# Mixture of experts behind an mLSTM: rows ahead of weights in the load queue, one transposition and one turn moved

## The chip, the core and the metric

The kernel runs on one core of a Trainium2 chip. A core has five engines that run side by side and wait for each other through semaphores: TensorE (PE in the rows; its weight loads are PEld), VectorE (DVE), ScalarE (ACT), GpSimd (POOL) and SyncE (SP), whose queue issues most of the transfers; 16 DMA engines carry them out. Each engine takes its instructions strictly in the order in which they were written. The metric is device time in microseconds (us); lower is better.

## What is computed

```python
def _moe_ref(x, token_ids, w1, w2):          # N, D, E, F = 3072, 320, 8, 1024
    expert_idx = token_ids * np.int64(2654435761) % np.int64(E)
    for e in range(E):
        mask = expert_idx == e
        xe = x[mask]
        h = np.maximum(xe @ w1[e], 0.0)
        out[mask] = h @ w2[e]
```

`x` (3072 tokens of 320) is the output of an mLSTM over 4 batches of 8 heads with 768 steps and head size 40. Everything is in 32-bit floats. The change lies wholly in the part with the experts.

## The kernel before, in words

The program has two parts. The first (0 to about 129 us) computes the mLSTM in 24 chunks of 128 tokens and writes the rows of `x` to a table in memory (`x_rows`); beside it the tokens are sorted by expert into index tables. The second part runs the eight experts, numbered here 0 to 7 as in the code, so that the fourth expert is expert 3.

An expert has 416 places for tokens: three blocks of 128 and a remainder of 32. Its rows take this way. `fetch(e)` gathers three blocks from `x_rows` with three indirect transfers that GpSimd issues (tile `xg`), and SyncE's queue stores them in a second table in memory (`x_slots`). `blocks(e)` loads them back as 12 small transfers on the same queue, in such an order that VectorE can turn rows into columns with one instruction, STREAM_TRANSPOSE in `turned(e)` (from tile `xb` to `xT`). The remainders of four experts are gathered at once, for experts 0 and 4. Expert 0 goes another way: its rows are transposed on TensorE in `turn` (two transpositions, a small VectorE copy at L891, a third transposition, then a copy out of the accumulators), the first two blocks already in the first part, the third block and the remainder in `turns0`.

`load_weights(e)` puts four transfers on SyncE's queue: `w1t`, two of `w1c`, `w2t`. The first layer of experts 1 to 7, `layer1_by_seven`, multiplies with seven products in place of eight and needs sums of weights (`sw`, by `sums_of_w1`, VectorE) and differences of rows (`tx`, by `sums_of_x`, VectorE); it works in two halves, `g` 0 and 2, and calls `meanwhile(g)` in the middle of each. The second layer takes the third block with `layer2` and the first two with `layer2_by_seven`, which calls its own `meanwhile` after its first four products. VectorE adds the partial results in both layers, ScalarE copies and applies the maximum, GpSimd scatters the results to the output.

The order of all work is that of the code: there is no scheduler in this part. SyncE's queue goes from top to bottom too, and a transfer that waits for a semaphore holds all that stand behind it. A block load waits until the store of its expert's rows has landed in memory.

The pools have `xg`, `xb`, `xT` and `tx` in two copies each, and the weights of the first layer in one early and two late places.

Of the kernel before, what the change touches and what calls it, by code (L numbers as in the profile page):

```python
# [22 lines left out]
def kernel(  # L23
# [30 lines left out]
    E, _, F = moe_w1.shape  # L54
    FB = F // P
# [32 lines left out]
    s_idx = consts.tile([P, NC], I32, name="s_idx")  # L88
# [25 lines left out]
    W = {}  # L114

    def load_weights(e, eng=None):

        W[e] = weights(moe_w1[e], moe_w2[e], wpools[e % 3 > 0], w2pools[e % 6 > 0], eng)
# [72 lines left out]
    with tc.tile_pool(name="gates", bufs=1) as gp, \  # L191
# [174 lines left out]
        def turn(s, what):  # L366
            d = st[s]
            d[what + "T"] = wk.tile([P, PR, P], F32, name=what + "T", bufs=3)
            tp = ps.tile([P, PR, P], F32, name="tr", tag="tr", bufs=2)
            for j in range(PR):  # L370
                nc.tensor.transpose(tp[:, j, :], d[what][:, 2 * j : 2 * j + 2, :].rearrange("p h d -> p (h d)"), ident[:])  # L371
            nc.scalar.copy(d[what + "T"][:], tp[:])
# [498 lines left out]
    def scatter(zp, idx, apart):  # L871
        zo = xp.tile([P, Dm], F32, name="zo", bufs=4)
        nc.scalar.copy(zo[:], zp[:])  # L873
        scatter_rows(zo, idx, apart)
# [111 lines left out]
                nc.scalar.activation(o, o, AF.Relu)  # L986
            done(g)

    def layer2(w, h, js, idx, apart, between=lambda j: None):
        for j in js:  # L990
            zp = mps.tile([P, Dm], F32, name="zp")
            for fb in range(FB):
                nc.tensor.matmul(  # L993
                    zp[:], lhsT=h[:, fb, j * P : (j + 1) * P], rhs=w[2][:, fb, :],
                    start=(fb == 0), stop=(fb == FB - 1),
                )
            scatter(zp, idx(j), apart)
            between(j)

# [56 lines left out]
    def cols_of(t, c0):  # L1056
        return lambda j: t[:, c0 + j : c0 + j + 1]

    with tc.manual_schedule():
        xTs, hrem, xbs = {}, {}, {}  # L1060
        xr0 = xp.tile([P, DB * P], F32, name="xr0", bufs=1)
        xTs[0] = xT0

        def fetch(e):
            if e == 0:
                gather(xg0[:, 2, :Dm], cols_of(g_idx, 0)(2))
                gather(xr0[:, :Dm], cols_of(g_idx, NR)(0))
            else:
                xg = xp.tile([P, NJ, Dm], F32, name="xg")
                for j in range(NJ):  # L1070
                    gather(xg[:, j], cols_of(g_idx, e * NJ)(j))
                nc.sync.dma_start(xs_d[e, :NM].rearrange("(t p) d -> p t d", p=P), xg[:])
            if e % EG == 0:
                if e:
                    xr = xp.tile([P, Dm], F32, name="xrg", bufs=1)
                    gather(xr[:], cols_of(g_idx, NR + e // EG)(0))
                else:
                    xr = xr0[:, :Dm]
                nc.sync.dma_start(xs_d[e : e + EG, NM:], xr[:])

        def blocks(e):
            xb = xbs[e] = xp.tile([P, CAP // 32, DB, 32], F32, name="xb")
            rows = xs_d[e].rearrange("(g j) d -> j g d", j=32)
            for q in range(4):
                for c in range(DB):
                    d0 = c * P + (q if c + 1 < DB else q % 2) * 32
                    nc.sync.dma_start(xb[q * 32 : (q + 1) * 32, :, c], rows[:, :, d0 : d0 + 32])  # L1087

        def turned(e):
            xT = xTs[e] = xp.tile([P, DB, CAP], F32, name="xT")  # L1090
            nc.vector.transpose(xT.rearrange("p c (g j) -> p g c j", j=32), xbs.pop(e)[:])

        def turns0():
            turn(xg0[:, 2], xT0[:, :, 2 * P : NM], False)
            remT = xp.tile([P, DB, P], F32, name="remT", bufs=1)
            turn(xr0, remT[:], True)
            nc.gpsimd.tensor_copy(xT0[:, :, NM:], remT[:, :, :RM])

        def rest(g):
            zp = mps.tile([P, Dm], F32, name="zp")  # L1100
            for fb in range(FB):
                for i in range(EG):
                    nc.tensor.matmul(  # L1103
                        zp[i * RM : (i + 1) * RM, :], lhsT=hrem[g][:, i, fb, :], rhs=W[g * EG + i][2][:, fb, :],
                        start=(fb == 0), stop=(fb == FB - 1),
                    )
            scatter(zp, cols_of(s_idx, NR + g)(0), True)

        fetch(0)
        fetch(1)  # L1110
        blocks(1)
        load_weights(1)
        h = h0
        for e in range(E):
            g, i = e // EG, e % EG
            if e + 2 < E:
                fetch(e + 2)
                blocks(e + 2)
                if e == 0:
                    load_weights(2)  # L1120
            if i == 0:
                hrem[g] = xp.tile([P, EG, FB, RM], F32, name="hrem")
            if e == 0:
                layer2(W[0], h, range(2), cols_of(s_idx, 0), True, lambda j: j == 0 and turns0())
                layer1(W[0], xT0, h, 2 * P, CAP, bank)
                turned(1)
                tx = sums_of_x(xTs[1])
            else:
                tw = differences_of_w2(W[e])
                sh = xp.tile([P, 4, FB // 2, P], F32, name="sh", bufs=1)  # L1130
                layer1_by_seven(
                    W[e], sw, xTs[e], tx, h, lambda g: g == 0 and 1 < e < E - 1 and turned(e + 1),
                    lambda g: sums_of_h(h, sh, g, nc.vector if g else nc.gpsimd),
                )
            nc.gpsimd.tensor_copy(hrem[g][:, i], h[:, :, NM:])
            layer2(W[e], h, (2,), cols_of(s_idx, e * NJ), True)
            if e + 1 < E:
                sw = sums_of_w1(W[e + 1])
            if i == EG - 1 and e + 1 < E:
                rest(g)  # L1140
            if e > 0:
                txs = []

                def meanwhile():
                    if e == 1:
                        turned(2)
                    if e + 1 < E:
                        txs.append(sums_of_x(xTs[e + 1]))

                layer2_by_seven(W[e], tw, h, sh, cols_of(s_idx, e * NJ), meanwhile)  # L1150
                tx = txs[0] if txs else None
            if e + 1 == E:
                rest(g)
            if e + 3 < E:
                load_weights(e + 3)

    nx = nc.values_load(xe[0:1, NX : NX + 1], min_val=0, max_val=NX)
    with tc.If(nx > 0):
        with tc.For_i(0, nx, 1) as k:
# [4 lines left out]
            w = weights(  # L1164
                moe_w1[bass.ds(ex, 1)].rearrange("e d f -> (e d) f"),
                moe_w2[bass.ds(ex, 1)].rearrange("e f d -> (e f) d"), wpools[0], w2pools[0],
            )
# [36 lines left out]
```

## Time and profile before

| | |
|---|---|
| three runs, median (lowest to highest) | 374.46 us (374.02 to 374.75) |
| profiled execution, own time | 372.34 us |
| its span, first to last instruction | 370.5 us |
| TensorE busy | 344.5 us, 93% of the span |
| VectorE, ScalarE, GpSimd busy | 59%, 37%, 57% of the span |
| mean granted TensorE clock | 0.979 of full speed |

The profiled execution is one run; 1.84 us of its time lie outside its span. All times inside the program, in the rows below too, are counted from the start of the span. A busy share is a mean over stages with different limits, so what a change is worth must be read in its own stage.

### The profile page before, as it was taken

Reading aid. Unit: us, or ns where it says so; the run is one execution under the profiler, and the core shown is the slowest. Engines: PE = TensorE matmul, PEld = TensorE weight load, DVE = VectorE, ACT = ScalarE, POOL = GpSimd, SP = SyncE. Lnnn points to the kernel's source line nnn. Section 1 sums busy time; section 2 is a strip of 40 time slices with the busy share of each in tenths; the row PEclk is TensorE's granted clock in tenths of the full one; section 3 lists DMA queues with packets and bytes.
Section 4 is the critical chain, followed back from the end, with each engine's and each line's share of the span. In section 5 each row is a group of like instructions: output and inputs, shape, how many; then the busy total and the mean of one; then the engine's idle time right before and its main releaser. Section 6 shows DMA issues by size and latency. Waiting matters only on the chain.

```text
span 370.5 us, 9233 instructions
## 1 busy us (share of the span) xinstructions
PE 344.5 (93%) x3595; PEld 296.8 (80%) x3595; DVE 219.8 (59%) x508; ACT 138.2 (37%) x325; POOL 209.5 (57%) x299
## 2 busy tenths in 40 slices
PE   8899999999999897999990999999999999999990
PEld 7777888888888775889880889869889899899870
DVE  7567897998878620185641565635575666745310
ACT  6476688767666611114110311410422413212300
POOL 8432778898884665149257315923944927419221
PEclk9999999999999999999996799999999999999997
DMA  7699999999999835788998959484478331000010
GB/s 148 116 185 171 169 185 203 206 184 181 172 210 239 253 90 177 176 285 181 317 309 160 308 118 323 105 225 156 118 155 260 104 68 37 1 18 35 6 46 5
DMA packets 162483, 59.35 MB, mean 160 GB/s; under 512 B 140130, under 2 KB 158206, under 8 KB 162438
## 3 DMA queue, kind: packets, MB, share of 16 engines
q1 hardware_dynamic: 158310, 49.07, 57.6%
q0 software_dynamic: 2832, 9.34, 7.8%
q8 instruction: 29, 0.48, 0.5%
q10 hardware_dynamic: 1296, 0.33, 0.4%
q14 instruction: 16, 0.13, 0.1%
HBM read 46.57 MB, written 12.48 MB: 159 GB/s over the span
## 4 chain that ended last, share of the span: by engine, by line
PE 76%; issue 5%; DMA 5%; DVE 4%; SPq 3%; POOL 3%; ACT 1%; POOLq 0%; ACTq 0%; DVEq 0%
PE mh L951 19%; PE mh L1025 11%; PE zp L993 9%; PE sp L419 7%; PE mh L959 6%; PE tr L371 6%; PE xh L477 5%; DMA x_slots<-xg 3%; PE xh L471 3%; PE ab L382 3%; PE xh L450 2%; SPq L1087 2%; POOL xg L110 1%; PE mh L157 1%; PE zp L1103 1%
## 5 line engine op out<-in xcount | busy, mean ns | idle before, releaser
L877 POOL DMA_INDIRECT out_dram<-zo,s_idx x26 | 26.7, 1027 | 86.8 <-issue 47.6
L993 PE MATMUL zp<-w2t,h 128*128 128x320 f32 x160 | 44.8, 433 | 0.5 <-issue 0.5
L951 PE MATMUL mh<-tx,sw 128*128 128x208 f32 x168 | 34.1, 354 | 10.1 <-DVE h L937 10.1
L951 PEld LDWEIGHTS mh<-tx,sw 128*128 128x128 f32 x168 | 31.1, 199 | 11.2 <-DVE h L937 11.0
L937 DVE TENSOR_TENSOR h<-u,mh 128x416 f32<-128x416 f32 (+1 forms) x56 | 25.2, 474 | 24.6 <-PE mh L951 16.5
L993 PEld LDWEIGHTS zp<-w2t,h 128*128 128x128 f32 x160 | 30.1, 190 | 12.0 <-issue 0.9
L477 PE MATMUL xh<-v,w 128*64 128x41 f32 x768 | 34.6, 222 | 0.0
L425 DVE TENSOR_TENSOR w<-sp,w 128x512 f32<-128x512 f32 x48 | 30.7, 681 | 4.8 <-ACT w L386 4.8
L386 ACT ACTIVATE w<-ab 128x512 f32<-128x512 f32 x48 | 26.1, 597 | 17.6 <-PE ab L382 17.6
L419 PE MATMUL sp<-qT,kT 64*128 64x128 f32 x384 | 29.8, 285 | 1.8 <-DVE w L425 1.2
L477 PEld LDWEIGHTS xh<-v,w 128*64 128x64 f32 x768 | 30.6, 138 | 0.0
L419 PEld LDWEIGHTS sp<-qT,kT 64*128 64x128 f32 x384 | 24.5, 187 | 6.7 <-issue 3.1
L110 POOL DMA_INDIRECT xg<-x_rows,g_idx x24 | 23.3, 972 | 9.0 <-issue 6.7
L1025 PE MATMUL mh<-tw,sh 128*128 128x160 f32 x168 | 27.4, 299 | 0.0
L471 PE MATMUL xh<-C,qs 128*64 128x82 f32 x320 | 27.3, 249 | 0.0
L494 POOL TENSOR_TENSOR x<-x,og 128x320 f32<-128x320 f32 x24 | 20.6, 864 | 7.5 <-ACT og L411 5.4
L937 DVE TENSOR_TENSOR u<-m,mh 128x416 f32<-128x416 f32 x28 | 16.2, 587 | 14.2 <-PE mh L951 7.7
L951 PE MATMUL mh<-xT,w1t 128*128 128x208 f32 x112 | 24.6, 342 | 0.0
L1025 PEld LDWEIGHTS mh<-tw,sh 128*128 128x128 f32 x168 | 24.3, 190 | 0.0
L959 PE MATMUL mh<-xT,w1c 64*128 64x208 f32 x224 | 24.1, 350 | 0.0
L975 ACT ACTIVATE h<-mh 128x416 f32<-128x416 f32 x14 | 7.2, 517 | 41.3 <-PE mh L959 41.3
L873 ACT COPY zo<-zp 128x320 f32<-128x320 f32 x12 | 5.1, 425 | 47.0 <-PE zp L993 30.5
(237 smaller groups left out, 765.6 us busy)
## 6 DMA issues: line engine op xcount, KB each, us to landing
w2t<-in_moe_w_dram SPq DMA_DIRECT2D x7, 1280.0 KB
w1t<-in_moe_w_dram SPq DMA_DIRECT2D x7, 1024.0 KB
xb<-x_slots SPq DMA_DIRECT2D x84, 52.0 KB
k<-in_k_dram SPq DMA_DIRECT2D x24, 160.0 KB
v<-in_v_dram SPq DMA_DIRECT2D x24, 160.0 KB
og<-in_o_gate_dram SPq DMA_DIRECT2D x24, 160.0 KB
q<-in_q_dram SPq DMA_DIRECT2D x23, 160.0 KB
x_slots<-xg SPq DMA_DIRECT2D x7, 480.0 KB
```

Of the source, the lines that this page charges most:

```text
L110: nc.gpsimd.indirect_dma_start(out=xg, out_offset=None, in_=x_d[:rows, :], in_offset=bass.IndirectOffsetOnAxis(ap=idx, axis=0),)
L386: nc.scalar.activation(w[:, hf], ab[:], AF.Exp)
L419: nc.tensor.matmul(sp[hf][:, j, :], lhsT=d["kT"][r, j, :], rhs=d["qT"][r, j, :], start=True, stop=True)
L425: nc.vector.tensor_tensor(d["w"][:, hf], d["sp"][hf][:], d["w"][:, hf], op=ALU.mult)
L471: nc.tensor.matmul(xh[t, 2 * j : 2 * j + 2, :], lhsT=d["qs"][:, j, t], rhs=Cs[b][c % 2][:, j].rearrange("p h d -> p (h d)"), start=True, s ...
L477: nc.tensor.matmul(hs[t, 2 * j + hf, :], lhsT=d["w"][:, hf, j, t], rhs=d["v"][:, 2 * j + hf, :], start=(c == 0), stop=True, skip_group_che ...
L877: ins = nc.gpsimd.indirect_dma_start(out=out[:, :], out_offset=bass.IndirectOffsetOnAxis(ap=idx, axis=0), in_=zo[:], in_offset=None, bound ...
L937: nc.vector.tensor_tensor(o, a, b, op=ALU.add)
L951: nc.tensor.matmul(pair(bank[n])[:, a], lhsT=lhsT(g + a), rhs=rhs, start=first and a == 0, stop=True, skip_group_check=True,)
L959: nc.tensor.matmul(pair(bank[n])[:, a], lhsT=w1c[k, g + a, :], rhs=xT[k, 2, r], start=False, stop=True, skip_group_check=True,)
L993: nc.tensor.matmul(zp[:], lhsT=h[:, fb, j * P : (j + 1) * P], rhs=w[2][:, fb, :], start=(fb == 0), stop=(fb == FB - 1),)
L1025: nc.tensor.matmul(bank[n], lhsT=lhsT(f), rhs=rhs(f), start=first and f == 0, stop=f == FB // 2 - 1, skip_group_check=True,)
```

## The change

Three things are written differently. In the loop over the experts, the weights of expert e + 2 are loaded at the top of iteration e, right behind the rows of expert e + 2; before, the weights of expert e + 3 were loaded at the end of iteration e, which is ahead of the rows of that expert. The rows of expert 3 are turned in the second layer of expert 2 (as those of expert 2 were in that of expert 1), no longer in its first layer. The transpositions of the first remainder stand between the sixth and the seventh matmul of expert 0's second block, no longer ahead of that block.

```diff
-    def layer2(w, h, js, idx, apart, between=lambda j: None):
+    def layer2(w, h, js, idx, apart, between=lambda j: None, within=lambda j, fb: None):
...
                     start=(fb == 0), stop=(fb == FB - 1),
                 )
+                within(j, fb)
...
-        def turns0():
+        def turn_third():
             turn(xg0[:, 2], xT0[:, :, 2 * P : NM], False)
+
+        def turn_rest():
             remT = xp.tile([P, DB, P], F32, name="remT", bufs=1)
             turn(xr0, remT[:], True)
             nc.gpsimd.tensor_copy(xT0[:, :, NM:], remT[:, :, :RM])
...
                 fetch(e + 2)
                 blocks(e + 2)
-                if e == 0:
-                    load_weights(2)
+                load_weights(e + 2)
...
-                layer2(W[0], h, range(2), cols_of(s_idx, 0), True, lambda j: j == 0 and turns0())
+                layer2(W[0], h, range(2), cols_of(s_idx, 0), True, lambda j: j == 0 and turn_third(), lambda j, fb: (j, fb) == (1, FB - 3) and turn_rest())
...
-                    W[e], sw, xTs[e], tx, h, lambda g: g == 0 and 1 < e < E - 1 and turned(e + 1),
+                    W[e], sw, xTs[e], tx, h, lambda g: g == 0 and 2 < e < E - 1 and turned(e + 1),
...
                 def meanwhile():
-                    if e == 1:
-                        turned(2)
+                    if e < 3:
+                        turned(e + 1)
...
-            if e + 3 < E:
-                load_weights(e + 3)
-
```

On SyncE's queue, from the weights of expert 2 on, stood before (`xg_2939` and `xb_2944` are the rows of expert 3, the three groups of `w1t`, `w1c`, `w2t` the weights of experts 2, 3 and 4):

```order
L97 DMA w1t_2815<-in_moe_w1_dram 128x2x1024
L100 DMA w1c_2816<-in_moe_w1_dram 64x4x128 x2
L101 DMA w2t_2817<-in_moe_w2_dram 128x8x320
L97 DMA w1t_2932<-in_moe_w1_dram 128x2x1024
L100 DMA w1c_2933<-in_moe_w1_dram 64x4x128 x2
L101 DMA w2t_2934<-in_moe_w2_dram 128x8x320
L1072 DMA x_slots<-xg_2939 128x3x320
L1087 DMA xb_2944<-x_slots 32x13x32 x12
L97 DMA w1t_3132<-in_moe_w1_dram 128x2x1024
```

At the same place of the queue stands now (`xg_2932` and `xb_2937` are the rows of expert 3, `w1t_2950` begins its weights, `xg_3132` and `xrg_3137` are the rows of expert 4 and the second remainder):

```order
L97 DMA w1t_2815<-in_moe_w1_dram 128x2x1024
L100 DMA w1c_2816<-in_moe_w1_dram 64x4x128 x2
L101 DMA w2t_2817<-in_moe_w2_dram 128x8x320
L1073 DMA x_slots<-xg_2932 128x3x320
L1088 DMA xb_2937<-x_slots 32x13x32 x12
L97 DMA w1t_2950<-in_moe_w1_dram 128x2x1024
L100 DMA w1c_2951<-in_moe_w1_dram 64x4x128 x2
L101 DMA w2t_2952<-in_moe_w2_dram 128x8x320
L1073 DMA x_slots<-xg_3132 128x3x320
L1080 DMA x_slots<-xrg_3137 4x32x320
```

The store and the 12 loads of expert 3's rows moved ahead of the four transfers of its weights; everything up to the weights of expert 2 stands where it stood.

On VectorE, in the first half of expert 2's first layer, stood before:

```order
L937 TENSOR_TENSOR u2_3171<-m1_3170,mh_3167 128x416
L937 TENSOR_TENSOR u4_3172<-m1_3170,mh_3168 128x416
L937 TENSOR_TENSOR u4_3172<-u4_3172,mh_3169 128x416
L1091 STREAM_TRANSPOSE xT_3185<-xb_2944 128x13x3x32
L937 TENSOR_TENSOR h0_74<-u4_3172,mh_3167 128x2x208
L937 TENSOR_TENSOR h0_74<-u2_3171,mh_3168 128x2x208
```

The transposition of expert 3's rows stands now in the second layer of expert 2, behind the sums of expert 3's weights and three additions:

```order
L908 TENSOR_TENSOR sw_3273<-w1t_2950,sw_3273 128x512
L1040 TENSOR_TENSOR u2_3283<-m1_3282,mh_3279 128x160
L1040 TENSOR_TENSOR u4_3284<-u2_3283,mh_3280 128x160
L1040 TENSOR_TENSOR zo_3286<-u4_3284,mh_3281 128x160
L1092 STREAM_TRANSPOSE xT_3307<-xb_2937 128x13x3x32
L912 TENSOR_TENSOR tx_3309<-xT_3307 128x208
L913 TENSOR_TENSOR tx_3309<-xT_3307,tx_3309 128x208
```

So the additions of the first layer (L937) no longer stand behind a wait for expert 3's rows. On TensorE, in the second layer of expert 0, the difference is (`xr_2768` is the first remainder, `xg_72` the third block):

```order
 L890 MATMUL tp<-ident,xg_72 128x128 x2
 L892 MATMUL tp<-ident,xg_72 128x128
+L993 MATMUL zp<-w2t,h_74 128x320 x6
 L890 MATMUL tp<-ident,xr_2768 128x128 x2
 L892 MATMUL tp<-ident,xr_2768 128x128
-L993 MATMUL zp<-w2t,h_74 128x320 x8
+L993 MATMUL zp<-w2t,h_74 128x320 x2
 L157 MATMUL mh<-xT_73,w1t 128x160 x4
```

Six of the eight matmuls moved ahead of the remainder's transpositions, and two are left between these and the first layer of the third block, which reads what they turn.

## Rows read from the trace of the kernel before

**Rows 1.** The page: the span.

```profile
span 370.5 us, 9233 instructions
```

**Rows 2.** The chain that ended last, two pieces: start us, us, what.

```profile
179.80 12.90 DMA x_slots<-xg
...
200.34 2.06 DMA xb<-x_slots
```

**Rows 3.** Timeline, TensorE: start us, us, operation, count [idle before <- releaser].

```profile
144.17 0.27 PE L892 MATMUL tp<-ident,xg 128*128 128x128 f32 x1
...
146.44 0.33 PE L892 MATMUL tp<-ident,xr 128*128 128x128 f32 x1 [1.78 <-DVE xr L891]
...
150.91 1.25 PE L157 MATMUL mh<-xT,w1t 128*128 128x160 f32 x8
...
161.45 0.87 PE L951 MATMUL mh<-xT,w1t 128*128 128x208 f32 x4
162.15 2.27 PE L951 MATMUL mh<-tx,sw 128*128 128x208 f32 x12
...
186.82 0.87 PE L951 MATMUL mh<-xT,w1t 128*128 128x208 f32 x4
...
204.49 4.09 PE L951 MATMUL mh<-tx,sw 128*128 128x208 f32 x12 [10.07 <-DVE h L937]
...
224.24 0.87 PE L951 MATMUL mh<-xT,w1t 128*128 128x208 f32 x4
```

**Rows 4.** Timeline, VectorE: the turn of expert 3, the weight sums and turn of 2.

```profile
179.40 0.69 DVE L905 TENSOR_TENSOR sw<-w1t 128x512 f32<-128x512 f32 x1 [1.45 <-DMA w1t<-in_moe_w_dram]
...
184.23 1.48 DVE L1091 STREAM_TRANSPOSE xT<-xb 128x1248 f32<-128x1248 f32 x1
...
202.48 1.48 DVE L1091 STREAM_TRANSPOSE xT<-xb 128x1248 f32<-128x1248 f32 x1 [12.06 <-DMA xb<-x_slots]
```

**Rows 5.** Stretches of 2 us: engines' busy time, granted clock, DMA share, GB/s.

```profile
core 0: us, PE busy (x) PEld busy (x) DVE busy (x) ACT busy (x) POOL busy (x), PEclk, DMA share, GB/s
...
200.00:202.00 2.00, 0.00 (x0) 0.00 (x0) 0.00 (x0) 0.00 (x0) 1.67 (x2) 0.50 0.73 109
```

**Rows 6.** Timeline, SyncE's queue: start us, us that the issuing took.

```profile
153.55 0.56 SPq L97 DMA_DIRECT2D w1t<-in_moe_w_dram  x1
...
156.20 0.87 SPq L1072 DMA_DIRECT2D x_slots<-xg  x1
166.13 6.02 SPq L1087 DMA_DIRECT2D xb<-x_slots  x12
172.20 0.47 SPq L97 DMA_DIRECT2D w1t<-in_moe_w_dram  x1
...
174.66 0.83 SPq L97 DMA_DIRECT2D w1t<-in_moe_w_dram  x1
...
179.80 4.73 SPq L1072 DMA_DIRECT2D x_slots<-xg  x1
194.72 6.09 SPq L1087 DMA_DIRECT2D xb<-x_slots  x12
200.92 0.41 SPq L97 DMA_DIRECT2D w1t<-in_moe_w_dram  x1
...
213.52 6.06 SPq L1087 DMA_DIRECT2D xb<-x_slots  x12
```

**Rows 7.** Timeline, all engines: around the turn of the first remainder.

```profile
145.43 0.56 DVE L896 COPY xT<-tp 128x384 f32<-128x384 f32 x1 [6.77 <-PE tp L890]
...
146.12 0.26 DVE L891 COPY xr<-xr 128x64 f32<-128x64 f32 x1
...
146.80 0.48 ACT L894 COPY remT<-tp 128x384 f32<-128x384 f32 x1 [0.93 <-PE tp L892]
147.35 0.26 POOL L1097 COPY xT<-remT 128x96 f32<-128x96 f32 x1 [0.17 <-issue]
...
159.96 0.69 DVE L905 TENSOR_TENSOR sw<-w1t 128x512 f32<-128x512 f32 x1
```

## The prediction, made before the changed kernel ran

> **What bounds the kernel now.** I read the chain of work that ended last first. In the part with the experts it is TensorE nearly everywhere, with one large hole: it leaves TensorE for a store of gathered rows that takes 12.90 us to land, and comes back by a block load that lands 2.06 us after its issue [rows 2]. The reader is to see that the hole belongs to transfers and not to any engine's work. Then I read TensorE in time. It stands still for 1.78 us ahead of the remainder's last transposition in expert 0, and for 10.07 us in the first layer of expert 2; between the start of expert 1 (161.45) and that of expert 2 (186.82) lie 25.37 us, between that of expert 2 and that of expert 3 (224.24) 37.42 [rows 3]. Expert 1 does the same work as expert 2, so expert 2 loses 12.05 us, of which 10.07 are the hole and 1.82 come behind it: the first twelve products after it take 4.09 us where the same twelve of expert 1 take 2.27 [rows 3], since the granted clock is then at 0.50, the 1.2 GHz level [rows 5]. It fell inside the hole, in which TensorE did nothing from 194.42 on.
>
> VectorE says why: it waits 12.06 us in front of the transposition of expert 3's rows [rows 4], and the additions that would free TensorE's accumulators stand behind it. SyncE's queue says why the rows are late. Expert 3's store is issued at 179.80, behind the weights of experts 2 (from 172.20) and 3 (from 174.66); its block loads can start only at 194.72, when the store has landed, and take 6.09 us to issue [rows 6]. They are in place 1.67 us later, at 202.48 [rows 4].
>
> **The rows ahead of the weights.** Nothing moves on SyncE's queue up to the weights of expert 2 at 172.20, and nothing in that stretch waits for TensorE. The store then takes the place of expert 3's weights, 174.66. It still has one expert's weights ahead of it. This case is in the trace twice: weights from 153.55, a store behind them at 156.20, block loads at 166.13, which is 12.58 us from the first weight to the landed store; and 200.92 to 213.52, 12.60 us, with a remainder's store as well [rows 6]. So the store lands at 172.20 + 12.6 = 184.8, the block loads are issued until 190.9 (6.1 us) and in place at 192.6 (1.7). The upper bound for the landing is the present 12.90 us counted from 174.66, hence 187.6.
>
> The weights of expert 3 now begin at 190.9 (193.7 at the upper bound), 16 to 19 us later than before. Who waits for them first is `sums_of_w1` on VectorE in expert 2. In expert 1 VectorE was ready for it at 179.40 - 1.45 = 177.95, 16.5 us after the expert's start [rows 3, 4]; in expert 2, started at 186.82 less the 1.0 us won below, that is 202.3. A first weight transfer lands within 6.4 us (issued at 153.55, read without a wait at 159.96 [rows 6, 7]) to 7.2 us (172.20 to 179.40, with the next expert's weights pressing behind it [rows 4, 6]). So it is in place at 198.1, or 200.9 with both upper bounds: 4.2 or 1.4 us in hand. I take no cost. What hides it is TensorE's work in expert 2's first layer; without that cover each microsecond is lost in full, because the additions of the second layer stand behind the sums.
>
> The Trainium skill, "DMA: Bandwidth & Descriptors", section "Rules for kernel authors", advises to issue a DMA early and to wait for it late, which speaks against this step for the weights. By its fit in "Anatomy of one DMA" (2 us and the bytes over 436 GB/s) a load of 1024 KB would take an estimated 4.4 us, landing at 195.3: no cost either. The first rival below is what the advice warns of.
>
> **The turn of expert 3 in the second layer.** One VectorE instruction of 1.48 us [rows 4] moves from between the additions of the first layer to behind three additions of the second. Expert 1 already has such a turn there, at 184.23, 22.8 us after its start, and it takes the plain 25.37 us; so I cost it at nothing. It is hidden by the rest of the second layer's products. Behind it stand the four differences `tx` of expert 3 and two output additions; if the rows were not in place, TensorE would wait in expert 3's second group of products. They are wanted at 185.8 + 22.8 = 208.6 and there at 192.6: 16 us in hand. Even with the order of the transfers unchanged (202.48) the turn would find its rows; each of the two edits alone removes most of the hole.
>
> Sum of both: expert 2 takes expert 1's 25.37 us instead of 37.42, a gain of **12.05 us** (the hole, the slow clock behind it, and 0.16 us of VectorE's turn in the first layer).
>
> **The remainder's turn.** Now TensorE waits 1.78 us for the small copy at 146.12 [rows 3, 7]. Eight matmuls of the block lie between 146.44 and 150.91 with a transposition, so 0.54 us each [rows 3]. Six of them in front give VectorE 3.2 us, and the copy is done by then, in 146.38. The gain is at most 1.78 us. But VectorE's copy ahead of it began only at 145.43, 1.0 us after the record of the third block's last transposition ends (144.44) [rows 3, 7], and no row says what held it. If that also holds the matmuls, the gain is 146.44 - 145.43 = 1.0 us. On the other side, TensorE's next reader needs the remainder copied by ScalarE (to 147.28) and GpSimd (to 147.61), 0.84 us behind the last transposition at 146.77 [rows 3, 7]; two matmuls, 1.1 us, cover that where eight did. If GpSimd is just issuing a transfer, the cover breaks and up to 1 us goes. A third limit stands in expert 1: VectorE reads its first weights at 159.96 without a wait, but when they landed between 153.55 and then isn't shown, and their issue isn't moved; at worst the gain ends there. So 0 to 1.78; I take **1.0**, the value that the unexplained release points to.
>
> **Sum.** 12.05 + 1.0 = 13.05 us. The span of 370.5 [rows 1] becomes 357.45, the profiled execution's 372.34 becomes 359.3. The median of the runs shown, 374.46, lies 2.1 us above that execution; taken off it, the forecast is **361.4 us**. All later experts keep their time: from 224.24 on TensorE has no hole to win.
>
> **Rivals.**
> *The weights come late.* The sums of expert 3's weights take over the wait of the turn. For it: they are the tightest point, and were loaded an expert earlier until now. Against: 4.2 us in hand, by two equal cases. It decides when the store lands after 189.0; a landing at 192.7, as late as now, would cost 3.7 us: 365.1. Chance 0.12.
>
> *The wait moves to expert 4's rows*, which are still turned in a first layer. Turns there are wanted 3.6 us after the expert's start (202.48 - 12.06 = 190.42 against 186.82 [rows 3, 4]), so at 224.24 - 13.05 + 3.6 = 214.8. Their store stands behind expert 3's weights: 190.9 + 12.6 = 203.5, and 7.8 for the loads makes 211.3. In hand 3.5 us; with the late landing above, 0.7. If these stores take 5 us more, 1.5 us are lost: 362.9. Chance 0.06.
>
> *It does not do what it says*: the store stays blocked until the DMA engines are free of all weights, lands where it did, and the hole only changes its name. That would need both the sums and the turn to wait as long as now, which the two slacks speak against: 374.5. Chance 0.02.
>
> *Slower.* Each expert's weights now stand behind a store's landing and 12 loads, so the queue becomes a ring: weights, store, loads, 172.20 to 190.9, 18.7 us a round against TensorE's 25.37. It decides above 25.4 us; to lose the 13.05 gained and 0.75 more over the five experts 3 to 7, a round must take 25.4 + 2.8 = 28.2 us, half as long again as the rows show: 375.2 or more. Chance 0.03.
>
> **How the numbers follow.** The forecast's own range is 360.2 (both gains full, less the 0.4 us by which the runs differ) to 362.8 (no early gain), chance 0.77. To this come the two rivals of partial loss, up to 365.5; the low end goes to 359.0 for waits that also shrink when fewer weights press (VectorE's 1.45 us at 179.40). The range 359.0 to 365.5 leaves out about 0.1. Faster by over 0.2% (about what a measurement here can tell from no change) are the forecast and the first two rivals, 0.95; within 0.2% 0.02; slower 0.03.
>
> **What would show it.** Expert 2 takes 25.4 us between its first matmuls, with the granted clock at 1.00 throughout; the store of expert 3's rows is issued near 174.7 and its loads near 185; no wait of VectorE in front of expert 3's turn, which stands in the second layer; the weight sums of expert 3 start without a wait for `w1t`. Ahead of the remainder's last transposition the idle 1.78 us are gone, and expert 1 starts near 160.5. I am wrong if VectorE waits for `w1t` in expert 2, for `xb` in expert 3, or if TensorE waits for the remainder's copy before the third block's first layer.

## The result: 362.0 us, 0.967 of before, and the profile after

The changed kernel took 362.01 us (median of four runs, 361.77 to 362.46) beside 374.27 (374.02 to 374.75) for the kernel before, measured beside it: a ratio of 0.9672, 95% interval 0.9656 to 0.9689. Forecast were 361.4, and 359.0 to 365.5 as the range. Lines of the kernel after stand up to three lower than before (the turn L1091 is now L1092, a store L1072 is L1073).

The page of the profile after; the third line is the granted clock of TensorE in 40 slices of the span, in tenths:

```profile
span 360.0 us, 9233 instructions
PE 344.1 (96%) x3595; PEld 295.7 (82%) x3595; DVE 221.5 (62%) x508; ACT 138.7 (39%) x325; POOL 210.0 (58%) x299
PEclk9999999999999999999999999999999999999997
```

TensorE's work is what it was (344.1 us busy); its idle time fell from 26.0 to 15.9 us, and every slice but the last is at 0.9 of full clock or more. TensorE in time, the rows that answer to [rows 3] (a matmul of the code is two rows of the trace, so the six matmuls ahead of the remainder are x12):

```profile
144.92 3.40 PE L993 MATMUL zp<-w2t,h 128*128 128x320 f32 x12
148.15 0.38 PE L890 MATMUL tp<-ident,xr 128*128 128x128 f32 x2
148.37 0.27 PE L892 MATMUL tp<-ident,xr 128*128 128x128 f32 x1
...
160.18 0.87 PE L951 MATMUL mh<-xT,w1t 128*128 128x208 f32 x4
161.72 2.38 PE L951 MATMUL mh<-tx,sw 128*128 128x208 f32 x12 [0.68 <-DVE sw L907]
...
186.50 0.87 PE L951 MATMUL mh<-xT,w1t 128*128 128x208 f32 x4
...
197.14 0.97 PE L951 MATMUL mh<-xT,w1t 128*128 128x208 f32 x4 [0.41 <-ACT m L965]
...
213.27 0.87 PE L951 MATMUL mh<-xT,w1t 128*128 128x208 f32 x4
```

The wait of 1.78 us at the remainder is gone, and so is the hole of 10.07. Expert 2 takes 213.27 - 186.50 = 26.77 us where it took 37.42, but not the 25.37 forecast; expert 1 takes 26.32 and not 25.37. SyncE's queue, answering to [rows 6]:

```profile
173.13 0.47 SPq L97 DMA_DIRECT2D w1t<-in_moe_w_dram  x1
...
175.66 1.03 SPq L1073 DMA_DIRECT2D x_slots<-xg  x1
184.49 6.10 SPq L1088 DMA_DIRECT2D xb<-x_slots  x12
190.69 0.52 SPq L97 DMA_DIRECT2D w1t<-in_moe_w_dram  x1
```

Store, loads and weights come as worked out (174.7, 184.8, 190.9). VectorE, the rows that answer to [rows 4], and two that are new:

```profile
159.65 0.69 DVE L905 TENSOR_TENSOR sw<-w1t 128x512 f32<-128x512 f32 x1 [0.69 <-DMA w1t<-in_moe_w_dram]
...
194.29 0.59 DVE L937 TENSOR_TENSOR h<-u,mh 128x416 f32<-128x416 f32 x1 [2.50 <-PE mh L951]
...
205.27 0.68 DVE L905 TENSOR_TENSOR sw<-w1t 128x512 f32<-128x512 f32 x1
...
210.68 1.48 DVE L1092 STREAM_TRANSPOSE xT<-xb 128x1248 f32<-128x1248 f32 x1
```

Neither the sums of expert 3's weights (205.27) nor the turn of its rows (210.68) waits. New are a wait of 0.69 us for expert 1's first weights, and a late addition in expert 2, 7.79 us after its start; in expert 1 of the trace before the same addition comes at 6.22.

### The profile page after: what moved, and what is told of

It reads as the page before. It is cut to its first block, busy times and chain, and to the rows that moved or that the text cites. A ratio compares the mean times of both kernels' runs of the same rounds, so it can differ in the third digit from the quotient of the medians.

```text
span 360.0 us, 9233 instructions
## 1 busy us (share of the span) xinstructions
PE 344.1 (96%) x3595; PEld 295.7 (82%) x3595; DVE 221.5 (62%) x508; ACT 138.7 (39%) x325; POOL 210.0 (58%) x299
## 4 chain that ended last, share of the span: by engine, by line
PE 75%; DMA 7%; issue 5%; DVE 5%; SPq 3%; POOL 2%; ACT 2%; POOLq 0%; DVEq 0%; ACTq 0%
PE mh L951 20%; PE mh L1026 13%; PE zp L993 8%; PE mh L959 6%; PE sp L419 6%; PE tr L371 5%; PE xh L477 4%; DMA xg<-x_rows,g_idx 3%; PE xh L471 3%; PE ab L382 3%; PE xh L450 2%; PE un L725 2%; SPq L1088 2%; DMA w1t<-in_moe_w_dram 1%; PE zp L1106 1%
## 5 line engine op out<-in xcount | busy, mean ns | idle before, releaser
L937 DVE TENSOR_TENSOR h<-u,mh 128x416 f32<-128x416 f32 (+1 forms) x56 | 25.5, 475 | 28.1 <-PE mh L951 19.7
L951 PE MATMUL mh<-tx,sw 128*128 128x208 f32 x168 | 33.0, 343 | 1.0 <-DVE sw L907 0.7
L951 PEld LDWEIGHTS mh<-tx,sw 128*128 128x128 f32 x168 | 29.4, 190 | 2.6 <-DVE h L937 1.7
L937 DVE TENSOR_TENSOR u<-m,mh 128x416 f32<-128x416 f32 x28 | 16.1, 587 | 13.7 <-PE mh L951 6.8
L959 PEld LDWEIGHTS mh<-xT,w1c 64*128 64x128 f32 x224 | 19.8, 186 | 3.5 <-issue 3.5
```

Of the source, the lines that this page charges most:

```text
L937: nc.vector.tensor_tensor(o, a, b, op=ALU.add)
L951: nc.tensor.matmul(pair(bank[n])[:, a], lhsT=lhsT(g + a), rhs=rhs, start=first and a == 0, stop=True, skip_group_check=True,)
L959: nc.tensor.matmul(pair(bank[n])[:, a], lhsT=w1c[k, g + a, :], rhs=xT[k, 2, r], start=False, stop=True, skip_group_check=True,)
```

## The experiments

The runs were made on three chips, e1 to e4 on chip 7, e5 to e8 on chip 10 and e9 to e12 on chip 15, each with runs of the kernel before beside them. That kernel's median went from 370.66 to 374.27 us, so a time is read beside it and not against the times that were expected. The time of an execution up to expert 0's second layer varied (below), so the table counts stages from their first matmuls, in one trace of each kernel: A from expert 0's second layer to the start of expert 2, then experts 2 and 3. Nothing but products makes 25.37 us in expert 2 and 30.01 in expert 3, in which the remainders' product of 4.51 stands.

| kernel | median us, before beside it | ratio (95%) | A | expert 2 | expert 3 |
|---|---|---|---|---|---|
| before, first trace | 374.27 | | 47.28 | 37.42 | 30.47 |
| after, first trace | 362.01, 374.27 | 0.967 (0.966 to 0.969) | 46.32 | 26.77 | 30.72 |
| e1 order only | 359.39, 371.92 | 0.968 (0.963 to 0.973) | 46.46 | 26.20 | 30.01 |
| e2 turn only | 367.43, 371.92 | 0.987 (0.981 to 0.993) | 46.31 | 25.37 | 37.42 |
| e3 remainder only | 370.47, 371.92 | 0.998 (0.995 to 1.002) | 46.54 | 37.64 | 30.01 |
| e4 without the remainder | 360.36, 371.92 | 0.968 (0.962 to 0.974) | 46.32 | 25.37 | 30.01 |
| e5 after, again | 358.04, 370.66 | 0.966 (0.962 to 0.970) | 46.63 | 25.37 | 30.01 |
| e6 all turns late, old order | 360.06, 370.66 | 0.969 (0.965 to 0.972) | 46.64 | 25.36 | 30.02 |
| e7 weights of 1 first | 359.27, 370.66 | 0.968 (0.964 to 0.972) | 45.68 | 25.37 | 30.01 |
| e8 the same, all turns late | 359.68, 370.66 | 0.969 (0.965 to 0.972) | 48.40 | 25.37 | 30.01 |
| e9 before, again | 373.42, 373.63 | 1.000 (0.996 to 1.004) | 47.50 | 36.22 | 30.58 |
| e10 gathers late | 358.50, 373.63 | 0.962 (0.957 to 0.967) | 46.20 | 25.37 | 30.01 |
| e11 loads twice | 363.54, 373.63 | 0.976 (0.970 to 0.981) | 45.92 | 27.66 | 30.84 |
| e12 loads three times | 371.81, 373.63 | 0.997 (0.994 to 1.000) | 46.13 | 30.41 | 38.37 |

**The parts alone.** e1 is the change without the two turns' edits:

```diff
-                layer2(W[0], ..., lambda j: j == 0 and turn_third(), lambda j, fb: (j, fb) == (1, FB - 3) and turn_rest())
+                layer2(W[0], ..., lambda j: j == 0 and (turn_third(), turn_rest()))
-                    W[e], sw, xTs[e], tx, h, lambda g: g == 0 and 2 < e < E - 1 and turned(e + 1),
+                    W[e], sw, xTs[e], tx, h, lambda g: g == 0 and 1 < e < E - 1 and turned(e + 1),
...
-                    if e < 3:
-                        turned(e + 1)
+                    if e == 1:
+                        turned(2)
```

> Only the order of the transfers is that of the change: each expert's rows are stored and loaded ahead of its weights. The fourth expert's rows are still turned in the first layer of expert 2, and the first remainder before its second block. Theory A (the hole was the queue's order, and the turn's new place is a second, smaller help): the turn is reached at about 190.4 us, where it stood in the trace before, while in the trace after the loads were issued from 184.49 to 190.69 and land about 1.7 us behind the last one; VectorE waits some 2 us there, the hole of 10.07 us shrinks to under 2, and the median is 363 to 365 us. Theory B (the turn's place carries the gain, the order only supports it): a hole of 8 us or more stays and the median is 371 or more.

Theory A, with a wait of VectorE of the size expected. VectorE of e1:

```profile
191.71 1.48 DVE L1092 STREAM_TRANSPOSE xT<-xb 128x1248 f32<-128x1248 f32 x1 [2.46 <-DMA xb<-x_slots]
```

The turn waits 2.46 us, TensorE 0.47 behind it, and expert 2 loses 0.83 in all. So the order alone is enough for nearly all of the gain; moving the turn is worth 0.83 us on top of it.

e2 keeps the old order (`load_weights(e + 3)` at the end of an iteration) and the remainder's old place, and moves the turn alone.

> Only the turn of the fourth expert's rows is moved, to the second layer of expert 2; the transfers keep the order of before. By the sentence on record that the turn would find its rows even so (they are there at 202.48, it wants them at 208.6), the hole goes and the median is about 363 us. The rival says that the sentence looked at one expert too few: with the old order the rows of expert 4 were stored and loaded after 213.52 and are there near 221.3, while its turn, which stays in the first layer of expert 3, would now come at about 215.5; the hole then moves one expert on and keeps some 5.8 us, and the median is 367 to 369.

The rival. VectorE and TensorE of e2, and a stretch behind the wait:

```profile
224.34 1.48 DVE L1092 STREAM_TRANSPOSE xT<-xb 128x1248 f32<-128x1248 f32 x1 [6.45 <-DMA xb<-x_slots]
```

```profile
226.34 4.53 PE L951 MATMUL mh<-tx,sw 128*128 128x208 f32 x12 [4.47 <-DVE h L937]
```

```profile
226.30:228.00 1.70, 1.66 (x5) 1.62 (x6) 1.05 (x3) 1.68 (x5) 1.70 (x3) 0.50 1.13 234
```

Expert 2 takes 25.37, and expert 3 gets the hole: its turn, still in the first layer, waits 6.45 us for the rows of expert 4. The hole of 4.47 costs 7.41 (37.42 less 30.01), mostly since the twelve products behind it run at a granted clock of 0.50 (the 1.2 GHz level) and take 4.53 us where they otherwise take 2.27.

e3 makes the remainder's edit alone, e4 all but this edit.

> Only the first remainder's turn is moved between the two products. Forecast on record for this part: 1.0 us of gain, so 373.2 to 373.4 beside 374.3 of before; the trace after shows 1.91 us gained in expert 0's second layer and 0.95 given back at the first additions of expert 1's weights, which wait 0.69 for their transfer. If the give-back belongs to the new order of the transfers and not to the weights of expert 1, this kernel gains 1.9 us (372.4). If the part gives nothing by itself, 374.3.

> The change without the remainder's turn: order of the transfers and fourth expert's turn as after, the remainder turned before the second block as before. If the parts add up, this is the time after (362.0) plus the 1.0 us that the record puts on the remainder's turn: 363.0 us. If the first additions of expert 1's weights wait for nothing here (no 0.69), the limit by that transfer is what cut 1.9 down to 1.0; if they wait as in the trace after, the remainder's turn was worth 1.9 and 364 comes out.

e3 can't be told from before (0.998), and e4 lies where the change does. The stages say why: A is 46.54 with the remainder's edit alone and 46.31 to 46.46 without it (e1, e2, e4), so the edit is worth nothing on this chip. What it wins ahead of expert 1 (20.00 us in e3 from expert 0's second layer to expert 1, 20.95 in e4) it gives back there: expert 1 takes 26.54 in e3, where TensorE waits 0.91 for the additions of its weights, and 25.37 in e4. So the give-back does not need the new order. The 1.0 us between the first two traces is another thing: the kernels with the old place wait 0.82 there, not 1.78. TensorE of e1:

```profile
145.12 0.33 PE L892 MATMUL tp<-ident,xr 128*128 128x128 f32 x1 [0.82 <-DVE xr L891]
```

**The change again, and other ways to the same end.**

> The changed kernel itself once more, unaltered. In its first trace expert 2 took 26.77 us, because VectorE's second addition came 7.79 us after the expert's start and not 6.22, and experts 3 to 5 took some 0.5 us more than 25.37 (with the 4.64 of the remainders' product in expert 3); in the kernel without the remainder's turn, whose instructions there are the same, expert 2 took 25.37 and every addition came at 6.22. Theory G (GpSimd's gathers, which are issued at that moment, hold the hand-over up whenever they are there): 26.8 again. Theory E (it belongs to the execution, not to the kernel): 25.4 in this or any later trace without it, and the part from expert 0's second layer to the end is 216 to 217 us in place of 219.8.

Theory E. VectorE of e5, whose expert 2 starts at 185.68:

```profile
191.91 1.36 DVE L937 TENSOR_TENSOR h<-u,mh 128x416 f32<-128x416 f32 x3 [0.93 <-PE mh L951]
```

The addition that came 7.79 us after the start comes at 6.23, under the same instructions, and expert 2 takes the 25.37 forecast. The 1.40 us that were missing in the first trace are no property of the kernel alone. (An addition or its release is called late below when VectorE starts later than in these rows: the second addition after 6.22 us.)

e6 is the kernel before with every turn in a second layer (`if e + 1 < E: turned(e + 1)` in `meanwhile`, none in the first).

> The kernel before with one edit: the rows of all experts, not of the second alone, are turned in the second layer; the transfers keep the order of before and the remainder is turned as before. Theory A (what was removed is the wait of a turn that is placed too early for its rows; a later turn and earlier rows are two ways to the same end): no turn waits, expert 2 takes 25.4 us, and the time is that of the change, 0.967 to 0.972 of before. Rival B (rows that are loaded behind the weights fall further behind with each expert): a wait of 3 us or more comes back at the turn of expert 4's or a later expert's rows, and the ratio is 0.975 or more.

Theory A: no turn waits in any expert, and expert 2 takes 25.36 and expert 3 30.02 with the transfers in the old order. So the new order and the later turn stand in for each other, if the turn is moved for all experts; for one expert alone (e2) it is not enough.

e7 issues the first transfer of expert 1's weights ahead of all stores of rows, e8 does so with all turns late:

```diff
+        w1t1 = first_of(moe_w1[1], wpools[1], nc.sync)
         fetch(0)
         fetch(1)
         blocks(1)
-        load_weights(1)
+        load_weights(1, None, w1t1)
```

> The change, with the first part of expert 1's weights (the 1024 KB that the additions read) put ahead of the stores of the remainder and of expert 1's rows on SP's queue. In the traces with the remainder's turn VectorE's additions for expert 1 wait 0.7 to 0.9 us for these weights, and expert 1 takes 26.3 to 26.5 us and not 25.37. Theory A (that transfer is the limit which cuts the remainder's turn down): the wait is gone, expert 1 takes 25.4, and the kernel gains 0.9 to 1.2 us on the change in the part from expert 0's second layer to expert 2's start (46.3 to 45.3). Rival B (the transfer only changes places with expert 1's rows, 1024 KB ahead of them): the turn of expert 1's rows, reached at 156.1, waits instead, 1 to 4 us, and the stage takes 46 to 49 us.

> The order of the change, its remainder's turn, all turns in the second layer, and expert 1's first weights ahead of the stores. If nothing but the product is left in the second to seventh expert, every expert takes 25.37 us (30.01 with the remainders' product in expert 3), and from expert 0's second layer to the end some 215.5 us, 1 us less than the change. If the turn in the first layer of experts 3 to 5 costs nothing where it stands, this kernel gains no more than the kernel with the weights moved alone.

VectorE of e7:

```profile
160.60 0.68 DVE L909 TENSOR_TENSOR sw<-w1t 128x512 f32<-128x512 f32 x1
```

The wait for `w1t` is gone, and A is 45.68 beside 46.63 of the change on the same chip: 0.95 us, as theory A has it. Expert 1 takes 25.69 where the change's takes 26.63, so that transfer is most of what takes the remainder's gain back; 0.32 us stay, not the 25.4 expected. From expert 0's second layer to the end e7 takes 215.94 us and the change 216.95, but the run as a whole is no faster (359.27 beside 358.04): the traced execution of e7 came to that layer at 141.76 and that of the change at 139.05. e8 was forecast too well: experts 1 and 2 take 25.37 us, but in its trace TensorE stood 4.04 us ahead of expert 0's second layer, where VectorE had waited 8.19 for the gathered rows, and ran the block behind it (sixteen rows) at a granted clock of 0.50 in 7.61 us in place of 4.6. The traced execution is the slowest of the six, 363.10 us where the others took 358.64 to 361.13. The transfer was issued at 128.59 there, ahead of that wait, which could be a collision of the two; against it stands e7, which issued the same transfer at 130.74 and whose VectorE waited 3.17 us for those rows, no longer than the change without it (3.40). No run settles it. Behind that layer e7 and e8 take the same 25.37 us for experts 2 and 4 to 6, so a turn in the first layer of experts 3 to 5 costs nothing there.

**The late additions, and the slack.** e10 is the change with all turns late, and with `fetch`, `blocks` and `load_weights` of expert e + 2 behind `differences_of_w2(W[e])`, so on GpSimd four additions of weights stand between an expert's scatters and the next gathers. e9 is the kernel before, unaltered.

> The kernel before itself once more, for its trace. In the first trace TensorE waited 1.78 us at the remainder's turn, and 0.81 to 0.82 in three later traces of kernels that turn it at the same place. If the 1.0 us between them belongs to the execution (VectorE's copy released late at 145.43), this trace shows 0.8 there as well, and from expert 0's second layer to expert 2's start 46.3 us and not 47.3: then moving the remainder's turn is worth nothing beside the 46.6 of the changed kernel's second trace. If it belongs to the kernel before, 1.8 and 47.3 again. The hole in expert 2 is 10 us in either case, and expert 2 takes 37.4 to 37.7.

> The change with all turns in the second layer, and with the gathers of the expert after next (and the stores and loads behind them) put behind GpSimd's differences of the second layer's weights, some 6 us later. If late hand-overs show in this call's other traces (second addition later than 6.22 us after an expert's start) and the gathers cause them, this kernel has none: every addition at 6.22 and 25.37 us an expert. If they show here too, the gathers aren't the cause. If the other traces have none, this one tells nothing of it, and only whether rows that are some 6 us later still arrive: by the chain in the second trace of the change the rows of expert 3 were loaded by 189.3 and wanted at 208.5, so no turn waits; its weights, loaded behind them, were there by 196.6 at the latest and read at 203.4, so they come just in time or up to 1 us late, and the time is that of the change or up to 1 us more.

On this chip VectorE was released late again. In e9 TensorE waits 2.00 us at the remainder, A is 47.50, and the second additions of experts 3 to 5 come at 6.88, 6.79 and 6.88. Expert 2 takes 36.22 us, less than the 37.4 to 37.7 expected, with a wait of 11.00 at the turn. By the words on record the 2.00 and 47.50 would belong to the kernel before. They don't: VectorE's copy ahead of the remainder's turn comes 1.0 to 1.4 us after TensorE's row has ended in e10, e11 and e12 too, which are versions of the change, and 0.1 us after it in all eight traces on chips 7 and 10, also in e6, which has the code of before in that place. e10, then e5:

```profile
144.36 0.27 PE L892 MATMUL tp<-ident,xg 128*128 128x128 f32 x1
145.96 0.56 DVE L896 COPY xT<-tp 128x384 f32<-128x384 f32 x1 [7.10 <-PE tp L892]
```

```profile
143.68 0.27 PE L892 MATMUL tp<-ident,xg 128*128 128x128 f32 x1
144.04 0.56 DVE L896 COPY xT<-tp 128x384 f32<-128x384 f32 x1 [5.87 <-PE tp L892]
```

So the lateness goes with the chip or the occasion, and where it is there the remainder's edit gains: A is 45.92 to 46.20 in e10 to e12, 1.3 to 1.6 us less than in e9.

e11, which has the gathers where the change has them, shows the late addition in expert 2; VectorE and GpSimd of e11:

```profile
190.68 0.59 DVE L937 TENSOR_TENSOR h<-u,mh 128x416 f32<-128x416 f32 x1 [1.11 <-issue]
194.55 0.59 DVE L937 TENSOR_TENSOR h<-u,mh 128x416 f32<-128x416 f32 x1 [3.28 <-PE mh L951]
```

```profile
187.29 1.00 POOL L877 DMA_INDIRECT out_dram<-zo,s_idx  x1 [6.68 <-issue]
188.59 0.98 POOL L877 DMA_INDIRECT out_dram<-zo,s_idx  x1 [0.31 <-issue]
189.87 1.00 POOL L110 DMA_INDIRECT xg<-x_rows,g_idx  x1 [0.30 <-issue]
191.17 0.98 POOL L110 DMA_INDIRECT xg<-x_rows,g_idx  x1 [0.30 <-issue]
192.46 0.95 POOL L110 DMA_INDIRECT xg<-x_rows,g_idx  x1 [0.30 <-issue]
193.71 0.95 POOL L110 DMA_INDIRECT xrg<-x_rows,g_idx  x1 [0.30 <-issue]
```

The addition comes 8.58 us after the expert's start (185.97), while the last of the six indirect transfers is being issued. In e10 the same four gathers stand apart; GpSimd and VectorE of e10, expert 2 started at 185.93:

```profile
188.55 0.98 POOL L877 DMA_INDIRECT out_dram<-zo,s_idx  x1 [0.31 <-issue]
189.54 1.57 POOL L912 TENSOR_TENSOR tw<-w2t 128x640 f32<-128x640 f32 x1
...
195.89 1.01 POOL L110 DMA_INDIRECT xg<-x_rows,g_idx  x1
197.20 0.97 POOL L110 DMA_INDIRECT xg<-x_rows,g_idx  x1 [0.30 <-issue]
198.47 0.94 POOL L110 DMA_INDIRECT xg<-x_rows,g_idx  x1 [0.30 <-issue]
199.72 0.95 POOL L110 DMA_INDIRECT xrg<-x_rows,g_idx  x1 [0.30 <-issue]
```

```profile
192.15 1.35 DVE L937 TENSOR_TENSOR h<-u,mh 128x416 f32<-128x416 f32 x3 [0.93 <-PE mh L951]
...
198.88 1.35 DVE L937 TENSOR_TENSOR h<-u,mh 128x416 f32<-128x416 f32 x3 [0.98 <-PE mh L951]
```

Every second addition of experts 2 to 7 comes at 6.22, and experts 2 to 6 take 25.37 (expert 3 with the remainders' product 30.01). The additions at 198.88 fall into the issue of a gather and are not late. The same trace has the late copy of expert 0, behind eight gathers that were not parted, so its additions are not on time because the whole execution was free of the delay. So the gathers matter, but not by being issued at that moment: with the unbroken row of scatters and gathers parted, the delay is gone. This is one trace, and the edit also moves the stores, the loads and, for experts 4 to 6, the turns; expert 2 has no turn in its first layer in e11 either, so the turns aren't the cause there. e10 has the lowest ratio of all, 0.962; the change itself was not run on that chip, and the intervals of the two touch.

e11 and e12 repeat the loads of expert 3's rows (`blocks(3, xbs[3])`, once and twice more) ahead of expert 3's weights.

> The change with the 12 block loads of expert 3's rows issued twice, so that everything behind them on SP's queue, expert 3's weights first, comes some 6.05 us later (12 loads take 6.1 us of the queue). On record the weights had 4.2 us in hand: by that the additions of expert 3's weights would wait some 1.9 us and the kernel lose up to that. By the second trace of the change they have 6.8 us at least (issued 189.36, 7.2 us to land at most, read at 203.38): then nothing waits and the time stays within 0.5 us of the change.

> The same with the block loads of expert 3 issued three times, so that expert 3's weights come 12.1 us later. They would be there near 208.7 on the second trace's clock, 5.3 us after VectorE wants them, and behind the waiting addition stand VectorE's additions for expert 2's second layer, so TensorE stops: 5 us, and some 2 more at the slow clock as behind the hole of 4.47 in the kernel with the turn alone. By the bound on record (4.2 in hand) the wait is 7.9 us and the loss 9 or more. If the weights had over 12 us in hand, nothing.

In e11 the weights are issued at 196.88, 6.2 us later than in the change, and nothing waits for them; what expert 2 loses is the late addition above. The next in line is the turn of expert 4's rows, which waits 1.31 us at 218.55. VectorE of e12:

```profile
210.36 0.69 DVE L905 TENSOR_TENSOR sw<-w1t 128x512 f32<-128x512 f32 x1 [5.31 <-DMA w1t<-in_moe_w_dram]
...
228.37 1.48 DVE L1093 STREAM_TRANSPOSE xT<-xb 128x1248 f32<-128x1248 f32 x1 [8.53 <-DMA xb<-x_slots]
```

And TensorE of e12:

```profile
213.91 0.51 PE L1026 MATMUL mh<-w2t,sh 128*128 128x160 f32 x2 [2.44 <-DVE u L1040]
...
230.37 3.92 PE L951 MATMUL mh<-tx,sw 128*128 128x208 f32 x12 [6.54 <-DVE h L937]
```

In e12 the weights are issued at 204.27, 13.6 us later than in the change, and the sums wait 5.31: so 8.3 us were in hand, not the 4.2 on record. The loss was expected at 7 us, all of it behind the weights, and the medians give 8.3 against e11 (371.81 less 363.54). By the traces the weights are the smaller part: I counted one wait, and there are two. The sums' wait of 5.31 stops TensorE for 2.44 us, and expert 2 takes 2.75 us more than in e11. The late weights hold the queue up behind them, the rows of expert 4 come late too, VectorE waits 8.53 at their turn, TensorE 6.54, and expert 3 takes 7.53 us more. For one round, from 172.13 to 204.27, the queue was slower than TensorE; the next round, to 224.30, took 20.0 us again, and experts 4 to 6 take what they take in the first trace after. So e12 is back near the time before (0.997) by one late round; the rival on record as slower, in which every round is too long, was not made.

## Why the forecast held, point by point

**The rows ahead of the weights: right.** Store, loads and weights came within 1 us of the forecast times, and neither the turn of expert 3's rows nor a later one waits. e1 shows that this edit alone brings nearly all of the gain, and e6 that it is not the only way to it. The slack of the weights was put too small by half: VectorE reads them at 205.27 and not at 202.3, because expert 2 started 0.7 us later than forecast, its addition ran 1.4 us late, and VectorE's four sums of `h` ahead of the reading took 3.14 us where the same four take 2.27 in expert 1 of the trace before; and the weights land within 6.1 us (204.27 to 210.36 in e12), not 7.2. The 4.4 us that the prediction estimates from the fit in the Trainium skill ("DMA: Bandwidth & Descriptors", "Anatomy of one DMA") are short of this 6.1; that section gives the fit for transfers issued by GpSimd, and this one is SyncE's, beside others. That "each microsecond is lost in full" without the cover is too strong: 5.31 us of waiting for the weights stopped TensorE for 2.44 in e12.

**The turn in the second layer: right as an addition, wrong as an edit of its own.** Beside the new order it is worth 0.83 us (e1 against 25.37). The sentence that "each of the two edits alone removes most of the hole" is false for the turn: the working followed the rows of expert 3 to 202.48 and not those of expert 4, whose turn stays in a first layer. e2 shows the hole there, at a price of 7.41 us of the 12.05. The on-record rival of a wait that moves to expert 4's rows named the place, under the new order, where it didn't come true: the turn at 216.79 in the first trace after does not wait.

**The 12.05 us of expert 2: the mechanism right, the size right without the late addition.** The first trace shows 10.65 (37.42 less 26.77); 1.40 is missing, all of it between VectorE's release at 7.79 in place of 6.22 and the products behind it. In e5 the same kernel takes the 25.37.

**The remainder's turn, 1.0 us: met in the first pair of traces (A 47.28 and 46.32), but not by the working on record.** The 1.0 was to be what is left when the late release holds the matmuls too. It doesn't hold them: in the first trace after, the copy is late as well (146.66), the matmuls start at 144.92, and the way to expert 1 is shorter by 1.91 us (21.91 to 20.00). The third limit, expert 1's first weights, then takes 0.95 back. The release that "no row says what held" goes with the chip or the occasion: 1.78 and 2.00 us of wait in two traces of the kernel before, 0.82 where releases are on time. There the give-back, 1.17 us in e3 and 1.26 in e5, of which 0.94 go in e7, eats the whole gain, and the edit is worth nothing (A is 46.54 and 46.63 with it in e3 and e5, 46.31 to 46.64 without it). That the sum came to the 1.0 forecast is luck.

**The sum: close, partly by luck.** The spans of the two first traces differ by 10.5 us (370.5 and 360.0), not by 13.05: 10.65 in expert 2, 0.96 in A, less 0.41 in experts 3 to 5, whose additions are late in both traces and a little later in the second, less 0.64 by which the program came later to expert 0's second layer. The median of before lies 2 us above its traced execution and that of after only 0.2; the forecast took 13.05 off the median, and the medians differ by 12.26. So 2.5 us too much in the terms met 2 us that no trace shows.

**What stays open:** why the releases are late in all six traces of the first pair and of chip 15 and in none of chips 7 and 10, and whether it is GpSimd's issuing or the transfers it starts; e10 moved the stores and loads along with the gathers. A version with both the gathers apart and expert 1's first weights early was not run, nor e10 beside the change on one chip.

## What to carry to other kernels

When a turn waits for rows that stand behind weights on one queue, put first what is wanted first, and then follow the same wait for every later pass of the loop before calling one edit enough: the hole of 10 us came back as one of 4.5, one expert on. A hole costs more than its length, since the granted clock fell inside it (10.07 cost 12.05, and 4.47 cost 7.41). A stall with no row that explains it is no gain to count on: ask first what the next reader waits for, here a transfer that took back 0.95 to 1.26 us, all of the gain on the chips where nothing was late.

## What the runs showed of the hardware

**Late releases behind rows of indirect transfers.** In the first two traces and on chip 15, VectorE's second addition came late where GpSimd had issued scatters and gathers without a break: 4 in a row (expert 1 of e9) on time at 6.23; 5 in a row (experts 3 to 5) late by 0.5 to 0.8 us; 6 in a row (expert 2) late by 1.57 in the first trace after and 2.36 in e11 and e12. Behind the 8 gathers ahead of expert 0's second layer, VectorE's copy began 1.0 to 1.6 us after TensorE's row had ended in all six of these traces, e10 among them, and 0.1 us after it in the other eight. On chips 7 and 10 no release was late, with the same rows of transfers; where they were parted by other work (experts 2 to 6 of e10) none was late either. GpSimd's rows don't show how long a gather lasts: the Trainium skill, "Perfetto Trace Analysis", in its section "DMA Instruction — SWDGE (GPSIMD)", on transfers that GpSimd issues, says that such a row ends when the descriptors are written, not when the data has moved. The trace agrees: in e9 the last gather of expert 1's rows begins at 139.39 and takes 0.95, and the store that waits for it goes at 144.09.

**Additions beside GpSimd's.** VectorE's four sums of `h` (128x256 each) took 0.42, 0.76, 0.50 and 0.42 us in expert 1 of the trace before, where only the last of GpSimd's own sums and a copy ran beside them, and 0.96, 0.94, 0.83 and 0.83 in expert 2 of e5, where GpSimd added all the while. The rows go together; no run parts them.

**The time to expert 0's second layer varies.** The instructions up to there are the same in all kernels but e7 and e8, and it began at 139.05 (e5) to 143.59 (e4). Differences under 1% between runs on different chips, or between few runs on one, therefore say little here, and the stages behind that point were compared instead.
